# Keys two visits later, stacks loaded in parts and earlier deadlines in a hand-ordered attention stage

## The chip, the core and the metric

The kernel runs on one core of one Trainium2 chip, as one launch. The core has TensorE (PE, matrix products; its weight loads are listed as PEld), VectorE (DVE), ScalarE (ACT), GpSimd (POOL) and SyncE (SP), which here issues nearly all DMA transfers. The metric is device time in microseconds (us) of one execution. A time without the word profile is the median of several unprofiled runs; durations of single instructions come from one profiled execution.

## The reference: two spectral layers and two banded attention layers

A sequence of 2048 rows with 640 features passes through four residual layers: spectral, attention, spectral, attention. Each first normalises its input row by row.

- A spectral layer multiplies by the 640x640 cosine and sine matrices, then by the 2048x2048 ones, and keeps the real part.
- An attention layer computes queries, keys and values with one 640x1920 weight (32 heads of 20 features), scores scaled by 20^-0.5, a band mask (a row sees itself and the 255 rows before it), a softmax, the product with the values, and a 640x640 output product.

```python
x = x + _A_ref(_layernorm(x, axis=-1), ...)
x = x + _B_ref(_layernorm(x, axis=-1), B_wqkv, B_wo)
x = x + _A_ref(_layernorm(x, axis=-1), ...)
x = x + _B_ref(_layernorm(x, axis=-1), B_wqkv, B_wo)
# in _B_ref:
mask = (idx[:, None] - idx[None, :] >= 0) & (idx[:, None] - idx[None, :] < W)   # W = 256
p = _softmax(jnp.where(mask, q @ k.T * Dh ** -0.5, -1e9), axis=-1)
o = p @ v                     # then o @ wo
```

## The kernel before, in words

**Precision.** Every float32 operand is split into two float16 parts, and each product is made of three float16 products (high by high, high by low, low by high). That is why a projection of one tile is 15 matmuls: five slices of the 640 features, three products each.

**Stages.** The trace falls into four stretches: spectral layer 0 (to about 576 us), attention layer 0 (to about 1161 us), spectral layer 1 (to about 1670 us), attention layer 1 (to the end). The change touches the function `attention` (L806) and two helpers it uses.

**Blocks and visits.** Attention handles 8 blocks (b) of 256 rows. The loop at L1274 makes 128 visits, 16 to a block; visit G works on one 128-row tile and four heads. The code counts in half visits: `now[0] = 2 * G`, and r (0, 2, ... 30) is the place in the block. Below, k = r / 2 is the visit's number in its block, 0 to 15. After the last scores the loop runs on for a few tail visits, so that the delayed steps can finish.

**What one visit does**, in the order in which it is written:

1. `scores(G)` (L1090): queries by keys on PE into PSUM tile st.
2. `by_key(G - KEY_LAG)` (L1148): the transposed scores, keys by queries. They need the row maxima, which enter as two extra rows of the query stack.
3. ACT turns them into probabilities (L1171) in two halves, and POOL masks them (L1175, L1177).
4. `hand_on` (L1132), three visits after the scores of a pair: PE transposes the maxima, ACT copies them, and a DMA stores them to DRAM (htd). One visit later `take_tops` (L1142) loads them into the query stack: `qs<-htd` in the trace (`ks<-htd` for block 0, whose query stack lies in a buffer of that name).
5. `largest` (L1112): DVE masks the scores and takes the row maxima.
6. `values` (VALUE_LAG behind, L1184) and `back` (BACK_LAG behind, L1205): the product with the values, and the transposition back.
7. At the visit's end `run_unit` (L1035) runs one unit of filler work on PE, and a second one on some odd visits.

**Units** (L1003) are the projections that the stage needs anyway, one product of 15 matmuls each. Ten "qk" units make queries and keys of the next block (128x256 results, "narrow", in the trace `pf<-early,big` with 256 columns), four "v" units make the values of a block and four "out" units make the output product of a finished one (128x320 results, "wide", `pf<-big,early` and `pf<-bo,ot`). `next_unit` (L1016) prefers wide units on even visits and narrow ones on odd, then the earliest due; but when `2 * left() >= MUST_TO - r`, only units that the block must still finish come into question: its own values and the next block's queries and keys (`must`, L1066). L1333 runs a second unit on odd visits when `2 * left() > MUST_TO - r`, which is always so from r = 26 on, since MUST_TO is 26.

**Stacks.** The keys (KS) and the queries (QS) of a block lie as tall stacks in SBUF. A finished qk product is stored to DRAM (qkd) through `hold`, HOLD half visits later. After the fifth product of a stack, `load_stack` is held in the same way; it takes a buffer and calls `fill_stack` (L310): two small loads of constant rows (`onesd`, 16 KB each), then six loads of 160 KB from qkd. Key stacks share three large buffers with the first query stack (tag quad, L213), query stacks have two (L828). A buffer is free once the last `by_key` that reads it has run.

**Rows.** For each block the normalised rows are made ahead: `x<-x2d` loads two tiles, `rows_norm` (L969) normalises them in small steps (`slow_step`, at most three in two visits), and `rows_turn` (L979) transposes them by DMA into `proj.rows` (`early<-xs`). Units that need them count as ready TURN_LAG half visits after the issue. Finished outputs are turned likewise (`ot<-os`).

**Order.** While `in_turn` is set, matmuls on PE and loads on SP keep the order in which they are written (L118, L178). SP works through its queue in that order: a DMA that waits holds up every later one.

The lags and limits stand as constants at L44 to L57.

Of the kernel before, what the change touches and what calls it, by code (L numbers as in the profile page):

```python
# [40 lines left out]
LAST_STEPS = (1, 258)  # L41
LAST_FROM = 3
HAND_LAG = 3
KEY_LAG = 6  # L44
VALUE_LAG = 9
BACK_LAG = 10
STEPS = ((1, 2), (0, 2))
MUST_TO = 26
HOLD = 4
PIECES = 2  # L50
TURN_LAG = 8
UNIT = 384
ROOT = float(0x5F3759DF - (1 << 22) - (1 << 30))
M_UP = 2.0 ** 15
SHIFT = -20.0
TURN_STEPS = 8
NORM_STEPS = (0, 4)  # L57
ROW_STEPS = 3
STAGES = ((2, 4, 5, 6), (1, 3, 5, 6), (1, 3, 5, 6))
X_UP = 2.0 ** 10  # L60
# [8 lines left out]
def body(ctx: ExitStack, tc: tile.TileContext, x_in, cmat, whid, wqkv, wo, out):  # L69
# [237 lines left out]
    def new_stack():  # L307
        return new_quad("ks").bitcast(F16).rearrange("p (a b) -> p a b", a=NP)

    def fill_stack(t, b, w):  # L310

        for pi in range(2):
            load(t[64 * pi:64 * pi + 2], ones_d[w].rearrange("a (p t) -> a p t", p=NP))
        for pi in range(2):
            for r, part in enumerate((0, 1, 0) if w == 0 else (0, 0, 1)):
                v = qk_d[b][w][part].rearrange("(p two d) t -> two d p t", two=2, d=DH)[pi]
                r0 = 64 * pi + 2 + DH * r  # L320
                load(t[r0:r0 + DH], v)
# [51 lines left out]
    def spectral(layer, res_src, hidden, first):  # L373
        with ExitStack() as st:
# [359 lines left out]
            for r in range(NR):  # L734
# [22 lines left out]
                for j in range(NJ):  # L757
                    n = r * NJ + j
                    if first:
                        if (r, j) == (0, 1):  # L760
                            side.append(chain(keep_w(), b_max()))
                        if (r, j) == (1, 2):
                            side.append(chain(b_scale(), b_split(0, 15)))
                    if r == NR - 1 and j == 3:
                        early_qk = ahead(proj)
                        side.append(early_qk)
                    if r == NR - 1 and j == NJ - 1:
                        for _ in early_qk:
                            pass
                        RES[r, j] = load_res(r, j)  # L770
                        for k in (1, 0):
                            proj.stack[k] = new_stack()
                            fill_stack(proj.stack[k], 0, k)
# [12 lines left out]
                    with ExitStack() as order:  # L786
                        if j == 0 and r == 0 and first:
                            order.enter_context(tc.issue_after(hidden.last))
                        main_a(r, j)
                        if j:  # L790
                            main_c(r, j - 1)
                        main_b(r, j)
                    if r < NR - 1 and j in STAGES[r]:
                        k = STAGES[r].index(j)
                        s = RS * (r + 1) + k
                        turned_x(s)
                        if k < RS - 1:
                            turn_x(s + 1, 2)
                        z_stage(s)
# [6 lines left out]
    def attention(layer, proj, dst, final):  # L806
        with ExitStack() as st:
# [13 lines left out]

            KS, QS = {0: proj.stack[1]}, {0: proj.stack[0]}

            def load_stack(b, w):
                if w:
                    t = KS[b] = new_stack()
                else:
                    t = QS[b] = sb.tile([P, NP, QB], F16, tag="qs", name="qs", bufs=2)  # L828
                fill_stack(t, b, w)

            def proj_qk(b, w, ct):
                yield from proj.qk(b, w, ct)
                if ct == ND - 1:
                    hold(partial(load_stack, b, w))

            def proj_v(b, ti, n):
                j = 2 * b + ti
                if n == 0:
                    t = sb.tile([P, H * VS + 32 - VS], F32, tag="v", name="v", bufs=6)
# [74 lines left out]
                    yield from next_layer(i, x3)  # L914

            pieces = iter(())
            held = deque()

            def hold(f):
                held.append((now[0] + HOLD, f))  # L920

            def run_held(upto):
                while held and held[0][0] <= upto:
                    held.popleft()[1]()

            proj.held = hold
            slow, idle, handed, later = deque(), deque(), deque(), []

            def new_xs():
                while len(later) > 1:  # L930
                    later.pop(0)[1]()
                return keep.tile([P, 2, D], F16, tag="xs", name="xs", bufs=2)

            def run_later():
                while later and later[0][0] <= now[0]:
# [18 lines left out]
            def split_wo():  # L954
# [5 lines left out]
                for n in range(ND):  # L960
                    f, sc = fs.pop(0), wsc[:, 1:2]
                    nc.scalar.activation(bo[0][:, n], f, AF.Copy, scale=sc)
                    nc.vector.scalar_tensor_tensor(bo[1][:, n], f, sc, bo[0][:, n], op0=OP.mult, op1=OP.subtract)
                    if n + 2 < ND:
                        fs.append(keep.tile([P, D], F32, tag="res1", name="wst", bufs=2))
                        load(fs[-1], wo[:, n + 2])
                    yield

            def rows_norm(b, x2s):  # L969

# [45 lines left out]
            def next_unit(wide=None):  # L1016
                us = [u for u in fill if u.ready()]
                if not us:
                    return None
                if 2 * left() >= MUST_TO - now[0] % (2 * NP):  # L1020
                    us = [u for u in us if must(u)] or us
                us = [u for u in us if u.wide == wide] or us
                u = min(us, key=lambda u: u.due)
# [42 lines left out]
            def must(u):  # L1066
                b = now[0] // (2 * NP)
                return u.kind in (("v", b), ("qk", b + 1))

            def left():  # L1070
                return sum(must(u) for u in fill)
# [202 lines left out]
            for G in range(NS // 2 + 1):  # L1274
# [100 lines left out]
```

## Time and profile before

| what | value |
|---|---|
| median of 3 runs | 2233.31 us (2225.26 to 2235.92) |
| profiled execution, its own time | 2228.98 us |
| its span, first to last instruction | 2227.0 us |
| PE busy | 2041.7 us, 92% of the span |
| DVE, ACT, POOL busy | 1504.3, 1127.9, 1451.9 us |
| mean granted TensorE clock | 0.978 |

The page of the profile gives the busy time of each engine, the chain of work that ended last and the costliest groups of instructions. Further views of the same trace are used below: the waits of one engine by what ended them, the instructions in order of time, and the busy time in chosen stretches. A row such as `PE st L122 <- DMA qs<-qkd: 20.1, 9, 4.5` reads: PE, about to write st, stood idle until the DMA that fills the query stack from qkd had landed; 20.1 us in 9 waits, the longest 4.5 us. In a row of the timeline, `x15` is a run of 15 like instructions, and the square bracket is the idle time ahead of it with what ended it.

### The profile page before, as it was taken

The page shows a single profiled execution, that of the slowest core. Times are in us where ns is not written, and L with a number is a line of the kernel's source. Part 1 is how long each engine was busy: PE and PEld are TensorE (multiplying, and loading weights), DVE is VectorE, ACT ScalarE, POOL GpSimd, SP SyncE. Part 2 cuts the span into 40 slices and gives each one's busy share as a digit, 9 for nine tenths or more (in the row PEclk, how much of TensorE's full clock was granted, in tenths as well). Part 3 has the DMA queues.
Part 4 walks back from the last instruction along what each step waited for, and adds up shares of the span by engine and source line. Part 5 has one row for each costly group of instructions (what it writes and reads, how often), then busy time and mean ns, then how long its engine had stood idle before and what let it go on. Part 6 is the DMA issues. An engine that isn't in the chain of part 4 may idle for free.

```text
span 2227.0 us, 54358 instructions
## 1 busy us (share of the span) xinstructions
PE 2041.7 (92%) x21145; PEld 1475.5 (66%) x21145; DVE 1504.3 (68%) x3253; ACT 1127.9 (51%) x1971; POOL 1451.9 (65%) x2170
## 2 busy tenths in 40 slices
PE   7999999999979989988899999999998899989987
PEld 4667666767656666666666767767675666666754
DVE  8877768676757777655637767776856666667653
ACT  5444455443346666555554444443324565656644
POOL 5667688769446776655557777676765665667644
PEclk9999999999999999999999999999999899999999
DMA  7555565374544444344435455444754244453332
GB/s 252 188 199 171 181 214 198 145 287 149 128 88 106 115 101 102 88 94 93 134 122 174 149 167 173 158 165 167 267 147 94 66 95 97 107 119 75 82 70 61
DMA packets 280502, 311.00 MB, mean 140 GB/s; under 512 B 107572, under 2 KB 214836, under 8 KB 271156
## 3 DMA queue, kind: packets, MB, share of 16 engines
q1 hardware_dynamic: 279668, 306.88, 47.2%
q8 instruction: 165, 2.70, 0.5%
q14 instruction: 93, 0.76, 0.1%
q10 hardware_dynamic: 576, 0.66, 0.1%
HBM read 201.72 MB, written 83.46 MB: 128 GB/s over the span
## 4 chain that ended last, share of the span: by engine, by line
PE 58%; DVE 17%; DMA 11%; ACT 5%; issue 4%; POOL 3%; SPq 1%; DVEq 0%; POOLq 0%; ACTq 0%
PE pf L122 25%; PE y L122 10%; PE st L122 8%; PE x L122 7%; PE z L122 7%; DVE cc L521 4%; DMA qs<-qkd 4%; DVE m L1121 4%; ACT ptq L1171 3%; DMA qs<-htd 2%; DVE st L1120 2%; SPq L182 1%; DMA qkd<-early 1%; DMA res<-accd 1%; DVE lnt L147 1%
## 5 line engine op out<-in xcount | busy, mean ns | idle before, releaser
L122 PEld LDWEIGHTS <-cc 128*128 128x128 f16 x5376 | 524.6, 98 | 206.9 <-issue 6.8
L1171 ACT ACTIVATE ptq<-st,shift,alpha 128x768 f32<-128x768 f32 (+2 forms) x512 | 485.3, 950 | 295.3 <-PE st L122 243.0
L122 PEld LDWEIGHTS <-big 128*128 128x128 f16 x4320 | 421.8, 99 | 162.0 <-issue 57.5
L1120 DVE COPY_PREDICATED st<-mask,st 128x256 f32<-128x256 int32 x448 | 190.1, 424 | 280.7 <-PE st L122 276.9
L1121 DVE TENSOR_REDUCE m<-st 128x2 f32<-128x512 f32 (+1 forms) x512 | 342.7, 671 | 10.5 <-DVE r L1219 0.3
L122 PE MATMUL pf<-early,big 128*128 128x256 f16 x2400 | 296.0, 277 | 5.7 <-ACT ht L1138 5.3
L122 PE MATMUL pf<-big 128*128 128x320 f16 x1680 | 242.1, 302 | 26.5 <-DVE zc L280 16.5
L122 PE MATMUL y<-zc,cc 128*128 128x320 f16 x1728 | 262.8, 299 | 3.7 <-DVE pf L544 3.7
L1175 POOL TENSOR_SCALAR_AFFINE_SELECT ptq<-ptq 128x512 f32<-128x512 f32 x224 | 145.4, 649 | 138.2 <-ACT ptq L1171 137.9
L521 DVE SCALAR_TENSOR_TENSOR cc<-cs,cc 128x512 f16<-128x512 f32 x256 | 229.3, 903 | 0.0
L518 ACT ACTIVATE cc<-cs 128x512 f16<-128x512 f32 x256 | 149.1, 621 | 133.2 <-POOL cs L511 61.1
L122 PE MATMUL st<-ks,qs 62*128 62x128 f16 (+1 forms) x2016 | 132.5, 240 | 81.4 <-ACT ptq L1171 36.7
L1177 POOL TENSOR_SCALAR_AFFINE_SELECT ptq<-ptq 128x512 f32<-128x512 f32 x256 | 165.3, 646 | 51.2 <-ACT ptq L1171 51.2
L521 DVE SCALAR_TENSOR_TENSOR cc<-cq,cc 128x512 f16<-128x512 f32 x192 | 198.0, 1033 | 0.2 <-ACT cc L518 0.2
L122 PE MATMUL pf<-ptq,v 128*32 128x128 f32 (+1 forms) x3840 | 188.1, 335 | 0.4 <-DVE early L280 0.4
L122 PEld LDWEIGHTS <-qs 62*128 62x128 f16 x2016 | 86.0, 95 | 141.9 <-issue 125.6
L122 PE MATMUL z<-zc,cc 128*128 128x320 f16 x1152 | 177.7, 299 | 1.7 <-DVE res L544 1.7
L122 PE MATMUL x<-zc,cc 128*128 128x320 f16 x1152 | 178.8, 300 | 0.0
L1222 POOL CAST os<-o 128x160 f16<-128x160 f32 x128 | 42.2, 329 | 198.5 <-DVE o L1220 198.4
L585 POOL TENSOR_TENSOR res<-res,pf 128x320 f32<-128x320 f32 x64 | 78.1, 1220 | 137.2 <-DVE pf L544 132.8
L122 PE MATMUL pf<-big,early 128*128 128x320 f16 x960 | 147.1, 309 | 1.2 <-ACT ht L1138 1.1
L122 PEld LDWEIGHTS <-ks 62*128 62x128 f16 x3008 | 113.9, 97 | 47.8 <-issue 46.0
(135 smaller groups left out, 3363.7 us busy)
## 6 DMA issues: line engine op xcount, KB each, us to landing
cq<-in_cmat_dram SPq DMA_DIRECT2D x64, 1024.0 KB
accd<-res SPq DMA_DIRECT2D x96, 320.0 KB
res<-accd SPq DMA_DIRECT2D x96, 320.0 KB
x<-x2d SPq DMA_DIRECT2D x64, 320.0 KB
qkd<-early SPq DMA_DIRECT2D x160, 128.0 KB
ks<-qkd SPq DMA_DIRECT2D x108, 160.0 KB
qs<-qkd SPq DMA_DIRECT2D x84, 160.0 KB
x2d<-res SPq DMA_DIRECT2D x32, 320.0 KB
```

The costliest lines, as they stand in the source:

```text
L122: i = getattr(nc.tensor, what)(*args, **kw)
L147: ts(u, g, g, h, op0=OP.mult, op1=OP.mult)
L182: i = nc.sync.dma_start(out, in_)
L518: nc.scalar.activation(cc[m][:, 0], f, AF.Copy, scale=C_UP)
L521: nc.vector.scalar_tensor_tensor(cc[m][:, 1], f, C_UP, cc[m][:, 0], op0=OP.mult, op1=OP.subtract)
L585: nc.gpsimd.tensor_tensor(x1[:, hi], x1[:, hi], p1, op=OP.add)
L1120: nc.vector.copy_predicated(sp[:, :, 2 * P:3 * P], mask[:, None, :].to_broadcast([P, 2, P]), far)
L1121: topped[0] = nc.vector.tensor_reduce(TOP[n][:, pi, :, k], sp[:, :, c0:3 * P], axis=AX.X, op=OP.max).ins
L1171: nc.scalar.activation(o[:, pi], tps[pi][:, :, first * P:3 * P], AF.Sigmoid, bias=shift, scale=alpha[:, 0:1])
L1175: nc.gpsimd.affine_select(out=q[:, :, a0], in_=q[:, :, a0], pattern=[[0, 4], [-1, P]], base=0, channel_multiplier=1, compare_op=OP.is_gt, ...
L1177: ins = nc.gpsimd.affine_select(out=q[:, :, a0 + 2], in_=q[:, :, a0 + 2], pattern=[[0, 4], [1, P]], base=0, channel_multiplier=-1, compare ...
L1222: nc.gpsimd.tensor_copy(hi, o)
```

## The change

Lags and deadlines move, the loads of a stack are split, and some steps change place:

- KEY_LAG, VALUE_LAG and BACK_LAG grow by 2 (to 8, 11 and 12 visits). `hand_on` keeps its lag of 3, so the maxima have four visits instead of two between the issue of their load and their use. The last `back` of each layer comes two visits later.
- HOLD falls from 4 to 2 half visits; MUST_TO falls from 26 to 24, and to 20 in block 0 (FIRST_TO). The second unit on odd visits now needs a unit that must still be done.
- `fill_stack` is split: `ones_stack` takes the buffer and loads the constant rows; it is held from the first product of a stack on. `load_stack` only loads the six parts. Both are held until visit 8 of the block for stacks of blocks 3 to 7, and not for blocks 1 and 2. `run_held` runs every held step that is due, not only the first in line.
- TURN_LAG falls from 8 to 6. The x2 rows are loaded at visit 13 of the block before, `rows_norm` starts at visit 0 instead of 2, and the next rows' buffer is taken at visit 7 instead of 8.
- The v units of the next block are ready from the start of the block instead of from visit 8 on.
- In the last block of attention layer 0, the next layer's weights are fetched from visit 5 instead of 8 on.
- Buffers: v tiles 8 instead of 6; xs tiles 3 instead of 2, in another pool. `split_wo` spreads its steps.

```diff
-KEY_LAG = 6
-VALUE_LAG = 9
-BACK_LAG = 10
+KEY_LAG = 8
+VALUE_LAG = 11
+BACK_LAG = 12
-MUST_TO = 26
-HOLD = 4
+MUST_TO = 24
+HOLD = 2
+FIRST_TO = 4
-TURN_LAG = 8
+TURN_LAG = 6
-NORM_STEPS = (0, 4)
+X2_STEP = 26
+ROWS_STEP = 14
+HIDDEN_STEP = 10
...
-    def fill_stack(t, b, w):
+    def fill_ones(t, w):
         for pi in range(2):
             load(t[64 * pi:64 * pi + 2], ones_d[w].rearrange("a (p t) -> a p t", p=NP))
+
+    def fill_stack(t, b, w):
...
-            def load_stack(b, w):
+            def ones_stack(b, w):
                 if w:
                     t = KS[b] = new_stack()
                 else:
                     t = QS[b] = sb.tile([P, NP, QB], F16, tag="qs", name="qs", bufs=2)
-                fill_stack(t, b, w)
+                fill_ones(t, w)
+
+            def load_stack(b, w):
+                fill_stack((KS if w else QS)[b], b, w)
 
             def proj_qk(b, w, ct):
+                if ct == 0:
+                    hold(partial(ones_stack, b, w), 2 * NP * (b - 1) + 2 * KEY_LAG if b > 2 else 0)
                 yield from proj.qk(b, w, ct)
                 if ct == ND - 1:
-                    hold(partial(load_stack, b, w))
+                    hold(partial(load_stack, b, w), 2 * NP * (b - 1) + 2 * KEY_LAG if b > 2 else 0)
...
-            def hold(f):
-                held.append((now[0] + HOLD, f))
+            def hold(f, at=0):
+                held.append((max(now[0] + HOLD, at), f))
 
             def run_held(upto):
-                while held and held[0][0] <= upto:
-                    held.popleft()[1]()
+                for item in [h for h in held if h[0] <= upto]:
+                    held.remove(item)
+                    item[1]()
...
-                if 2 * left() >= MUST_TO - now[0] % (2 * NP):
+                if 2 * left() >= must_to() - now[0] % (2 * NP):
...
+            def must_to():
+                return MUST_TO - FIRST_TO * (now[0] < 2 * NP)
...
-                        fill.append(Unit(2 * NP * (b - 1) + 2 * VALUE_LAG - 2, proj_v(b, ti, n), ("v", b), 2 * NP * b + 2 * VALUE_LAG, ns=15 * 136))
+                        fill.append(Unit(2 * NP * (b - 1), proj_v(b, ti, n), ("v", b), 2 * NP * b + 2 * VALUE_LAG, ns=15 * 136))
...
-                if g < NG and b < NBQ - 2:
-                    if r == NORM_STEPS[0]:
-                        x2s = [keep.tile([P, D], F32, tag="res0", name="x2", bufs=2) for t in range(2)]
-                        for t in range(2):
-                            load(x2s[t], x2_d[2 * (b + 2) + t])
-                    if r == NORM_STEPS[1]:
-                        slow.append(rows_norm(b + 2, x2s))
-                if g < NG and r == 2 * VALUE_LAG - 2 * (VALUE_LAG % 2):
+                c = b + 2 + (r > 0)
+                if g < NG and c < NBQ and (g == 0 or r == X2_STEP):
+                    x2s = [keep.tile([P, D], F32, tag="res0", name="x2", bufs=2) for t in range(2)]
+                    for t in range(2):
+                        load(x2s[t], x2_d[2 * c + t])
+                if g < NG and c < NBQ and r == 0:
+                    slow.append(rows_norm(c, x2s))
+                if g < NG and r == ROWS_STEP:
                     flush(("v", b))
                     if b < NBQ - 2:
                         proj.new_rows(b + 2)
+                if g < NG and r == HIDDEN_STEP:
                     if b == NBQ - 1 and not final:
+                        flush(("v", b))
                         hidden = Hidden(xu_d)
...
-                if G % 2 and (g >= FULL_TO or g < NG and 2 * left() > MUST_TO - r):
+                if G % 2 and (g >= FULL_TO or g < NG and left() and 2 * left() > must_to() - r):
                     run_unit()
```

More of the change, by code (lines that the diff above doesn't have):

```diff
@@ L772, in spectral @@
                             proj.stack[k] = new_stack()
+                            fill_ones(proj.stack[k], k)
                             fill_stack(proj.stack[k], 0, k)
@@ L838, in proj_v @@
                 if n == 0:
-                    t = sb.tile([P, H * VS + 32 - VS], F32, tag="v", name="v", bufs=6)
+                    t = sb.tile([P, H * VS + 32 - VS], F32, tag="v", name="v", bufs=8)
                     nc.gpsimd.memset(t[:, :H * VS].rearrange("p (h e) -> p h e", e=VS)[:, :, DH:], 1.0)
@@ L916, in attention @@
             pieces = iter(())
-            held = deque()
-            def hold(f):
-                held.append((now[0] + HOLD, f))
+            held = []
+            def hold(f, at=0):
+                held.append((max(now[0] + HOLD, at), f))
             def run_held(upto):
-                while held and held[0][0] <= upto:
-                    held.popleft()[1]()
+                for item in [h for h in held if h[0] <= upto]:
+                    held.remove(item)
+                    item[1]()
             proj.held = hold
@@ L929, in new_xs @@
             def new_xs():
-                while len(later) > 1:
+                while len(later) > 2:
                     later.pop(0)[1]()
-                return keep.tile([P, 2, D], F16, tag="xs", name="xs", bufs=2)
+                return sb.tile([P, 2, D], F16, tag="xs", name="xs", bufs=3)
             def run_later():
@@ L963, in split_wo @@
                     nc.vector.scalar_tensor_tensor(bo[1][:, n], f, sc, bo[0][:, n], op0=OP.mult, op1=OP.subtract)
+                    for _ in range(3):
+                        yield
                     if n + 2 < ND:
@@ L966, in split_wo @@
                         load(fs[-1], wo[:, n + 2])
-                    yield
             def rows_norm(b, x2s):
```

## The prediction

> **What bounds the kernel now.** I read the page first, for the engine that carries the end.
>
> ```profile
> span 2227.0 us, 54358 instructions
> PE 2041.7 (92%) x21145; PEld 1475.5 (66%) x21145; DVE 1504.3 (68%) x3253; ACT 1127.9 (51%) x1971; POOL 1451.9 (65%) x2170
> ...
> PE 58%; DVE 17%; DMA 11%; ACT 5%; issue 4%; POOL 3%; SPq 1%; DVEq 0%; POOLq 0%; ACTq 0%
> PE pf L122 25%; PE y L122 10%; PE st L122 8%; PE x L122 7%; PE z L122 7%; DVE cc L521 4%; DMA qs<-qkd 4%; DVE m L1121 4%; ACT ptq L1171 3%; DMA qs<-htd 2%; DVE st L1120 2%; SPq L182 1%; DMA qkd<-early 1%; DMA res<-accd 1%; DVE lnt L147 1%
> ```
>
> PE leads, and 11% of the chain that ended last is DMA: the loads of the query stacks (qs<-qkd) and of the maxima (qs<-htd), which the change moves. What these cost PE itself is read from the waits of PE in the two attention stages; first stage 0 (575 to 1112 us), then stage 1 (1669 to 2190 us). Columns: total us, times, longest.
>
> ```profile
> PE st L122 <- ACT ptq L1171: 17.0, 25, 2.0
> PE st L122 <- DMA qs<-qkd: 16.3, 7, 3.0
> PE st L122 <- DMA qs<-htd: 11.0, 5, 3.1
> PE st L122 <- DMA ks<-htd: 5.1, 2, 4.6
> ...
> PE st L122 <- DMA x<-x2d: 4.5, 1, 4.5
> ```
> ```profile
> PE st L122 <- ACT ptq L1171: 23.0, 38, 2.0
> PE st L122 <- DMA qs<-qkd: 20.1, 9, 4.5
> PE st L122 <- DMA qs<-htd: 7.4, 7, 1.8
> PE st L122 <- DMA ks<-htd: 1.9, 1, 1.9
> ```
>
> PE waited for DMA 36.9 us in stage 0 (16.3 + 11.0 + 5.1 + 4.5) and 29.4 us in stage 1 (20.1 + 7.4 + 1.9): 66.3 us. The wait put down to x<-x2d is one at the first scores of a block, where a stack was due too, so I count it with the stacks.
>
> Next, where in a block they lie: PE in order of time around the start of block 3 of stage 1, and at visit 12 of that block.
>
> ```profile
> 1848.14 0.62 PE L122 MATMUL st<-ks,qs 62*128 62x128 f16 x8
> 1850.48 4.25 PE L122 MATMUL pf<-big,early 128*128 128x320 f16 x30
> 1854.66 0.28 PE L122 MATMUL st<-ks,qs 62*128 62x256 f16 x1
> 1858.42 0.69 PE L122 MATMUL st<-ks,qs 62*128 62x256 f16 x8 [3.48 <-DMA qs<-qkd]
> ...
> 1907.38 0.21 PE L122 MATMUL st<-qs,ks 62*128 62x128 f16 x1 [1.27 <-DMA qs<-htd]
> ```
>
> The first scores of a block wait for its query stack, and by_key of visit 12 waits for the maxima. What follows such a wait, and what a visit without one takes, is read from the busy time by stretches (columns: length, busy time of PE, PEld, DVE, ACT, POOL, granted clock, DMA share, GB/s):
>
> ```profile
> 1858.42:1864.41 5.99, 5.99 (x38) 3.72 (x40) 2.36 (x6) 1.98 (x2) 1.99 (x4) 0.50 1.17 269
> 1864.41:1868.86 4.45, 4.45 (x69) 3.02 (x69) 2.15 (x4) 2.84 (x5) 1.17 (x3) 0.98 0.09 32
> 1868.86:1872.11 3.25, 3.25 (x41) 2.37 (x40) 2.85 (x7) 1.98 (x2) 0.99 (x5) 1.00 0.02 6
> 1872.11:1876.19 4.08, 4.08 (x68) 3.06 (x69) 3.54 (x9) 2.41 (x4) 2.42 (x6) 1.00 0.22 81
> 1876.19:1879.44 3.25, 2.85 (x41) 2.38 (x41) 2.50 (x7) 2.42 (x4) 2.37 (x8) 1.00 0.01 1
> ...
> 575.80:1112.20 536.40, 474.34 (x6366) 345.62 (x6365) 356.98 (x858) 313.91 (x500) 325.02 (x718) 0.96 0.44 102
> 1669.50:2190.40 520.90, 465.00 (x6319) 339.84 (x6318) 336.30 (x799) 302.81 (x481) 314.61 (x708) 0.96 0.40 89
> ```
>
> After the 3.48 us wait the clock stood at 0.50 and the rest of the visit took 5.99 us; the same kind of visit undisturbed takes 3.25. The other rows price a clean visit: an even one 3.25 us with a wide or a narrow unit, an odd one 4.45 with a wide and 4.08 with a narrow. An odd visit with two wide units ran from 1848.14 to 1854.66, 6.52 us. So a visit is PE's, except that an even one doesn't fall below 3.25. A whole stage of 128 visits had a mean clock of 0.96: 8% of it at half speed, some 42 us of stage time each, of which at most half, 21 us, was lost.
>
> **The change, part by part.**
>
> *Maxima, keys at 8 visits.* The load of the maxima is issued at visit 4 after the scores' pair began; its use moves from visit 6 to 8, two visits or 7.33 us (4.08 + 3.25) later. The longest such wait above is 4.6 us, so all 25.4 us go (11.0 + 5.1 + 7.4 + 1.9). What is late next is the stack load.
>
> *Stack loads.* The queue of SP in order of time, around visits 14 and 15 of block 2, and a key stack with the maxima behind it:
>
> ```profile
> 1846.71 0.38 SPq L182 DMA_DIRECT2D qkd<-early  x1
> 1847.14 0.61 SPq L182 DMA_DIRECT2D qs<-onesd  x2
> 1848.58 3.11 SPq L182 DMA_DIRECT2D qs<-qkd  x6
> 1851.79 4.20 SPq L190 DMA_TRANSPOSE ot<-os  x1
> 1856.04 0.58 SPq L182 DMA_DIRECT2D x<-x2d  x1
> 1857.12 3.21 SPq L190 DMA_TRANSPOSE early<-xs  x2
> 1860.39 1.61 SPq L182 DMA_DIRECT2D x<-x2d  x2
> ...
> 1901.84 1.33 SPq L182 DMA_DIRECT2D qs<-htd  x2
> ```
>
> The query parts were issued from 1848.58 on and PE went on at 1858.42: 9.8 us to fill a stack. They started 1.87 us after the last store; the constant rows lie in that gap, beside the store's own landing, so loading them early gains little; I take nothing.
>
> When the last narrow unit falls, I worked out by hand from the unit rules. Before, products start at visit 3 in stage 1 and the last is at visit 12; HOLD puts the load at 14. After, rows are ready from visit 0. Units must be preferred once left() >= 12 - k. In blocks 1 to 3 the last product falls at visit 11, the load at 12, two visits (7.3 us) earlier than before: those waits (3.48 us at most of the kind quoted) go. In block 0, with its limit of 10 visits, the load moves to visit 11. From block 4 on, three or four value units of the block are still open at its start, since only six visits of a block are free for wide units and eight wide ones arise; the last product is then at visit 12 and the load at 13, one visit earlier. There it stands behind two x2 loads (0.8 us each of SP by the row of 1.61), and in stage 1 also behind the two row transposes (3.21 us), because norm steps there run two per odd visit, end at visit 11 and issue at 13. In stage 0 they issue at visit 9. From visit 13 to the next block are 4.45 + 3.25 + 4.45 = 12.2 us. The load starts after product, conversion and store: with 3 to 3.5 us, and 9.8 for filling, it lands at about 13, one us late in stage 0; in stage 1 it lands near 16 to 17, four us late. With the half clock behind it (about 2.7 us by the row of 5.99, in part) I price three boundaries at 1 us in stage 0 and at 4 us in stage 1: **15 us stay**. Bounds: 0, and 6 x (7.5 + 2.7) = 61 with the two waits of the worst boundary of before, 4.47 + 3.08:
>
> ```profile
> 2126.42 0.37 PE L122 MATMUL st<-ks,qs 62*128 62x256 f16 x1 [4.47 <-DMA qs<-qkd]
> 2129.87 0.69 PE L122 MATMUL st<-ks,qs 62*128 62x256 f16 x8 [3.08 <-DMA qs<-qkd]
> ```
>
> *A hold on SP in block 1.* The key stack of block 2 has no lower limit on its time (b > 2 is false), but three large buffers hold two key stacks and the first query stack, which by_key reads until visit 7 of block 1. Its constant rows are issued at visit 2 there, so SP stands until visit 7, and the stores and loads of maxima behind it are late by a visit or so: between nothing and 5.5 us per stage (the maxima issued at 1901.84 behind a stack landed at 1907.38). With the clock I take **3.5 us each, 7 us**.
>
> *Clock.* Of the 42 us lost at most in both stages, some is lost in visits without units (below) and stays. I take **30 us** gained, bounds 20 and 42. The Trainium skill ("TensorE: Matmul & The Clock Gate", Part 1) says that half rate follows an idle window of about 3.4 us and full rate a busy one. By it the short waits of visit 12 would cost no clock, and the gain would be some 20 us in place of 30. The trace speaks against a strict threshold: behind the wait of 1.27 us at 1907.38 a narrow unit of 15 took 2.93 us in place of 1.81:
>
> ```profile
> 1903.86 1.81 PE L122 MATMUL pf<-early,big 128*128 128x256 f16 x15
> ...
> 1908.51 2.93 PE L122 MATMUL pf<-early,big 128*128 128x256 f16 x15
> ```
>
> *Units.* The second units at visit 15 go (2.07 us each, 6.52 - 4.45, in seven blocks per stage). By the hand count 6 doubles are left per stage (two in block 0, two each in blocks 5 and 6, one of them an output forced at visit 12), where 7 were. That is a gain of 2 us per stage, **4 us**. Bounds: nothing, and 14 x 2.07 = 29.
>
> *The end of each stage.* Two more tail visits with keys but no scores. Two tail visits of stage 1 are the last two rows here:
>
> ```profile
> 2179.47:2182.72 3.25, 2.41 (x53) 1.76 (x53) 2.23 (x5) 2.18 (x4) 1.62 (x3) 1.00 0.02 4
> 2190.44:2192.11 1.67, 0.88 (x16) 0.63 (x15) 1.08 (x3) 1.04 (x2) 0.63 (x4) 1.00 0.08 32
> 2192.11:2194.87 2.76, 2.09 (x46) 1.34 (x46) 0.00 (x0) 2.21 (x3) 1.99 (x4) 1.00 0.26 101
> ```
>
> That is 1.67 + 2.76 = 4.43 us a stage, **9 us** added; what the two early visits that lose their keys save is left out, with zero as its lower bound. The first row is a visit of the last block without a unit: it takes 3.25 us all the same, so those visits give nothing back.
>
> *At nothing:* buffers and split_wo, hidden by PE; TURN_LAG 6, because a turned tile is used three visits (11 us) after its issue and a transpose held SP 4.20 us; if that cover fails, it costs the difference, one to two us a block. Weights fetched earlier lie beside PE's units.
>
> **Sum:** -66.3 - 30 - 4 + 15 + 7 + 9 = -69 us. The profiled execution itself took 2229 us (2 us around its span), so 2160 us. The median shown, 2233.31, lies 4 us above; I don't add that.
>
> **Rivals.**
>
> 1. *The stacks stay late.* If filling takes 9.8 us plus what now stands ahead, the eight boundaries that I take as cleared keep their wait, 36.4 / 14 = 2.6 us each, with 1.5 of clock: +33 us, 2193. For it: the SP rows, a queue that is full just there. Against it: two visits of lead in blocks 1 to 3.
> 2. *Everything clears.* No boundary left late, no hold: 2160 - 22, with more of the clock 2130. For it: clean visits of 3.25 and 4.45 follow at once after each wait.
> 3. *Slower: x2 loads and row transposes ahead of the stack at visit 13.* If every one of the 14 boundaries is late, each costs its wait and half clock in place of the gain; the 84 us between the forecast without its boundaries (2145) and the time of before are used up at 6 us a boundary. Landing 5 us after the first scores of a block decides; at 8 us late it would be 14 x (8 + 2.7) = 150, 2295. For it: row transposes, an output's transpose (4.20 us) and x2 loads may share the last three visits. Against it: in blocks 0 to 3 the load is issued before them. The Trainium skill ("DMA: Bandwidth & Descriptors", Queues, rings and completion order) says that each DMA engine takes descriptors in ring order, which is the ground for such a delay.
> 4. *No change:* ACT and DVE take the time that PE gains, since an even visit is at 3.25 us already. About 2225. Against it: odd visits are PE's, and the waits all lay ahead of clean visits.
>
> **How the numbers follow.** Forecast (2145 to 2175) 0.50; rival 2 (2115 to 2145) 0.17; rival 1 (2175 to 2215) 0.20; no change 0.05; slower 0.08. A measurement of this kernel tells about 0.5% from no change, 11 us. Faster by more: 0.50 + 0.17 + 0.20 = 0.87. The range leaves out rivals 3 and 4 and the ends of 1 and 2: 2118 to 2208, within the bounds of the unknown terms (the clock's 42, the boundaries' 61).
>
> **What would show it.** PE's waits for qs<-htd and ks<-htd near 0; waits for qs<-qkd only ahead of blocks 5 to 7, longer in stage 1; clean blocks 2 and 3 of about 59.4 us (8 x 3.25 + 6 x 4.08 + 2 x 4.45); an SP wait on PE in block 1; a mean clock over the stages of 0.98. Waits for qs<-qkd at every boundary would make it rival 1 or 3; waits on ACT in place of DMA, rival 4; a PE wait for early<-xs or ot<-os would show a cover that I counted as there.

## The result, and the profile after

| | before | after |
|---|---|---|
| median | 2233.12 us (2225.26 to 2240.04, 12 runs) | 2233.64 us (2228.35 to 2239.91, 12 runs) |
| span of the profiled execution | 2227.0 us | 2232.0 us |
| mean granted clock | 0.978 | 0.978 |

The ratio is 1.0002, with a 95% interval of 0.9986 to 1.0019: no change that a measurement can tell. 69 us were forecast to go.

The page after; the last line is the chain of work that ended last:

```profile
span 2232.0 us, 54291 instructions
PE 2038.7 (91%) x21145; PEld 1470.8 (66%) x21145; DVE 1507.8 (68%) x3253; ACT 1127.5 (51%) x1971; POOL 1448.6 (65%) x2170
...
PE pf L125 26%; PE y L125 10%; PE st L125 7%; PE x L125 7%; PE z L125 6%; DVE cc L523 5%; DMA qs<-qkd 4%; DVE m L1134 3%; ACT ptq L1184 3%; SPq L185 2%; DVE st L1133 2%; DMA qkd<-early 2%; DMA ks<-qkd 2%; DMA res<-accd 1%; DVE lnt L150 1%
```

The maxima (qs<-htd) are gone from the chain; the query stack (qs<-qkd) is not. The waits of PE after, in attention stage 0 (575 to 1165 us) and then in stage 1 (1669 to 2232 us), as total, times, longest:

```profile
PE st L125 <- DMA qs<-qkd: 20.4, 7, 8.4
PE pf L125 <- DMA ot<-os: 5.4, 1, 5.4
...
PE st L125 <- DMA qs<-htd: 1.9, 3, 1.1
```
```profile
PE st L125 <- DMA qs<-qkd: 23.2, 8, 4.7
PE pf L125 <- DMA early<-xs: 3.9, 2, 3.1
PE pf L125 <- DMA ot<-os: 2.7, 1, 2.7
...
PE st L125 <- DMA qs<-htd: 1.1, 1, 1.1
```

Waits for the maxima fell from 25.4 to 3.0 us. Waits for the stacks did not fall: 20.4 and 23.2 us, where they were 16.3 and 20.1, the longest 8.4 us in place of 4.5. Two covers that the prediction counted on failed: turned tiles (ot<-os) and turned rows (early<-xs) now hold PE.

The same, read from stretches of the kernel after (length, busy time of PE, PEld, DVE, ACT, POOL, clock, DMA share, GB/s). The first two rows are the scores' part of each stage (first to last visit with scores), the next two are block 2 of stage 0 and of stage 1:

```profile
578.00:1104.93 526.93, 467.46 (x6321) 340.01 (x6321) 358.15 (x857) 309.42 (x495) 320.91 (x708) 0.97 0.46 104
1669.20:2187.25 518.05, 461.67 (x6262) 337.22 (x6262) 337.94 (x797) 298.83 (x476) 310.51 (x700) 0.95 0.39 88
...
701.53:761.60 60.07, 58.38 (x857) 43.76 (x856) 49.59 (x126) 41.14 (x63) 44.56 (x97) 0.99 0.42 87
1786.94:1846.90 59.96, 58.17 (x858) 43.67 (x858) 45.00 (x108) 40.51 (x62) 43.13 (x96) 0.99 0.40 85
```

Blocks 2 are as forecast. Over both scores' parts, though, PE's idle time (length less busy) went only from 118 us before to 116. What fails lies at the **boundaries**: visit 15 of a block with visit 0 of the next. Some of the seven in each stage of the kernel after (the second, the fifth and sixth of stage 0; the third, the fifth and the last of stage 1); the sum row is over all 14:

```profile
689.65:705.10 15.45, 10.10 (x108) 6.41 (x107) 5.08 (x13) 4.39 (x6) 3.77 (x10) 0.78 0.82 178
...
881.58:903.64 22.06, 10.83 (x108) 6.77 (x108) 6.13 (x14) 4.39 (x6) 5.76 (x13) 0.69 0.74 186
959.11:972.41 13.30, 9.55 (x108) 6.11 (x109) 5.72 (x13) 4.39 (x6) 5.76 (x13) 0.87 0.73 150
...
1842.51:1850.14 7.63, 7.63 (x108) 5.36 (x108) 4.66 (x11) 5.27 (x8) 4.14 (x11) 1.00 1.18 239
...
1968.71:1986.60 17.89, 9.95 (x107) 6.57 (x108) 5.72 (x13) 4.39 (x6) 5.33 (x13) 0.71 0.74 146
...
2113.51:2129.24 15.73, 10.56 (x107) 6.82 (x108) 5.72 (x13) 4.39 (x6) 5.76 (x13) 0.78 0.67 127
sum 184.63, PE 126.05 PEld 81.96 DVE 78.37 ACT 63.26 POOL 64.35; mean PE 9.00 PEld 5.85 DVE 5.60 ACT 4.52 POOL 4.60
```

A clean boundary takes 7.63 us (the row at 1842.51), so 14 would take 107. They take 184.6; before, the same 14 stretches took:

```profile
sum 194.80, PE 150.09 PEld 101.48 DVE 73.95 ACT 71.55 POOL 64.61; mean PE 10.72 PEld 7.25 DVE 5.28 ACT 5.11 POOL 4.62
```

Ten us gained, where the forecast had 194.8 - 107 - 15 = 73. And these ten are not waits: PE is busy 24 us less there, for the second units of visit 15 run elsewhere now, and its idle time grew from 44.7 to 58.6. The 63 us are most of what is missing. The two tails took some more: from the last scores to the end of the kernel it is 44.79 us after (2187.25 to 2232.04) and 36.58 before, and stage 0's end grew by 7.0 us (557.3 to 564.3 us up to the first scores of stage 1).

How a boundary gets late shows in SP's queue of the kernel after, around visit 13 of block 4 in stage 1 (visit 13 begins at 1960.98), and in what PE does then:

```profile
1963.54 2.45 SPq L185 DMA_DIRECT2D x<-x2d  x2
1966.04 3.17 SPq L193 DMA_TRANSPOSE early<-xs  x2
1969.31 0.62 SPq L185 DMA_DIRECT2D qkd<-early  x1
1971.73 3.02 SPq L185 DMA_DIRECT2D qs<-qkd  x6
```
```profile
1970.95 2.21 PE L125 MATMUL pf<-bo,ot 128*128 128x320 f16 x15
1977.85 0.37 PE L125 MATMUL st<-ks,qs 62*128 62x256 f16 x1 [4.69 <-DMA qs<-qkd]
1981.47 0.69 PE L125 MATMUL st<-ks,qs 62*128 62x256 f16 x8 [3.25 <-DMA qs<-qkd]
...
1983.32 3.35 PE L125 MATMUL pf<-big,early 128*128 128x320 f16 x15
```

The last store of the stack (qkd<-early) went out behind the x2 loads and row transposes, 8.3 us after visit 13 began, and the load 2.4 us behind it, 1.4 us before PE had nothing left (1973.16). The stack comes in two halves: a wait of 4.69 us for the first, 3.25 us for the second, and then 15 matmuls take 3.35 us in place of 2.21.

Not every late boundary has these loads ahead. The last three boundaries of each stage are all late; three of these six (the sixth and seventh of stage 0, the seventh of stage 1) have neither x2 loads nor row transposes in SP's queue from visit 13 to the load, and still took 13.3, 12.6 and 15.7 us. The queue at the last of them, where visit 13 begins at 2105.89:

```profile
2109.21 0.38 SPq L185 DMA_DIRECT2D qkd<-early  x1
2113.53 3.22 SPq L185 DMA_DIRECT2D qs<-qkd  x6
```

The last store went out 3.3 us after visit 13 began, and the load 4.3 us behind it (2.5 us behind it at the other two). With some 9.7 us to fill a stack, that is more than the 12 us from visit 13 to the next block, even without them ahead.

### The profile page after: what moved, and what is told of

Its sections match the earlier page's. It is cut to its first block, busy times and chain, and to the rows that moved or that the text cites. A ratio compares the mean times of both kernels' runs of the same rounds, so it can differ in the third digit from the quotient of the medians.

```text
span 2232.0 us, 54291 instructions
## 1 busy us (share of the span) xinstructions
PE 2038.7 (91%) x21145; PEld 1470.8 (66%) x21145; DVE 1507.8 (68%) x3253; ACT 1127.5 (51%) x1971; POOL 1448.6 (65%) x2170
## 4 chain that ended last, share of the span: by engine, by line
PE 57%; DVE 16%; DMA 11%; ACT 5%; issue 4%; POOL 3%; SPq 3%; DVEq 0%; POOLq 0%; ACTq 0%
PE pf L125 26%; PE y L125 10%; PE st L125 7%; PE x L125 7%; PE z L125 6%; DVE cc L523 5%; DMA qs<-qkd 4%; DVE m L1134 3%; ACT ptq L1184 3%; SPq L185 2%; DVE st L1133 2%; DMA qkd<-early 2%; DMA ks<-qkd 2%; DMA res<-accd 1%; DVE lnt L150 1%
## 5 line engine op out<-in xcount | busy, mean ns | idle before, releaser
L1134 DVE TENSOR_REDUCE m<-st 128x2 f32<-128x512 f32 (+1 forms) x512 | 342.5, 671 | 10.7 <-DVE st L1133 0.5
L125 PE MATMUL pf<-early,big 128*128 128x256 f16 x2400 | 289.8, 274 | 7.9 <-ACT ht L1151 4.3
L125 PE MATMUL pf<-big 128*128 128x320 f16 x1680 | 242.0, 302 | 28.3 <-DVE zc L283 16.7
L125 PEld LDWEIGHTS pf<-ptq,v 128*32 128x32 f32 x3840 | 112.6, 111 | 44.1 <-issue 3.5
## 6 DMA issues: line engine op xcount, KB each, us to landing
qkd<-early SPq DMA_DIRECT2D x160, 128.0 KB
```

Of the source, the lines that this page charges most:

```text
L125: i = getattr(nc.tensor, what)(*args, **kw)
L1134: topped[0] = nc.vector.tensor_reduce(TOP[n][:, pi, :, k], sp[:, :, c0:3 * P], axis=AX.X, op=OP.max).ins
```

## The experiments

Three theories for the late boundaries: **order** (the load stands in SP's queue behind x2 loads and row transposes), **deadline** (a last product at visit 12 is one visit too late), **hold** (with HOLD 2, SP comes to a store before POOL has converted the product, and stands: SP waited 116.4 us for POOL's early tiles after, 38.9 before). Beside them stand the shorter TURN_LAG and the lags. A ratio is to the kernel before, with its 95% interval; unless said otherwise an edit is to the kernel after.

### The lags alone, on the kernel before

```diff
-KEY_LAG = 6
-VALUE_LAG = 9
-BACK_LAG = 10
+KEY_LAG = 8
+VALUE_LAG = 11
+BACK_LAG = 12
...
-                    t = sb.tile([P, H * VS + 32 - VS], F32, tag="v", name="v", bufs=6)
+                    t = sb.tile([P, H * VS + 32 - VS], F32, tag="v", name="v", bufs=8)
```

> The kernel before with the three lags alone raised by 2 (and 8 value tiles in place of 6). If the lag does what the trace of after suggests, the 25.4 us of waits for the maxima go to under 3 us and the two stage ends grow by 8 us each: 2233 - 25 - 5 (clock) + 16 = about 2219 us. Rival, the boundary takes it: the stack loads are met with the time that the maxima gave, the waits for qs<-qkd grow from 36 to over 50 us and the time stays at 2233.

Measured: 2245.78 us, ratio 1.0040 (1.0025 to 1.0054), slower than either expectation. PE's waits for the query stacks in stage 0 and in stage 1 of this kernel:

```profile
PE st L122 <- DMA qs<-qkd: 16.7, 8, 3.7
...
PE st L122 <- DMA qs<-qkd: 36.0, 11, 7.5
```

No wait for the loads of maxima is left (one of 4.7 us is put down to a store of theirs), and the waits for stacks stand at 16.7 and 36.0 us, where they were 16.3 and 20.1. In stage 1 a visit that no longer waits for its maxima brings PE sooner to a boundary whose stack comes no sooner. Removing one of two waits in a row is worth little while the second is set by DMA. The tails are the other part: they are 10.7 and 9.2 us longer than before (568.0 and 45.8 us).

### The change without the lags

```diff
-KEY_LAG = 8
-VALUE_LAG = 11
-BACK_LAG = 12
+KEY_LAG = 6
+VALUE_LAG = 9
+BACK_LAG = 10
```

> The changed kernel with the old lags (6, 9, 10), all else as changed. If the lag is a gain, the maxima are waited for again and the ends shrink: 2234 + 25 + 5 - 16 = about 2248 us. If the longer ends eat the lag (rival), it is 2234 or below, and the waits for the maxima stay small because stacks now load at other visits.

Measured: 2250.40 us, ratio 1.0053 (1.0033 to 1.0073). PE's waits for qs<-htd in stage 0, then in stage 1:

```profile
PE st L125 <- DMA qs<-htd: 23.2, 11, 4.8
...
PE st L125 <- DMA qs<-htd: 30.1, 9, 5.2
```

With 15.3 us more for ks<-htd (9.9 and 5.4), maxima cost 68.6 us and stacks 15.1: the same exchange from the other side. Within the change the lags are worth some 11 us (1.0053 to 1.0002).

### The stack loads ahead of the x2 loads

```diff
+                if g < NG and r == X2_STEP:
+                    run_held(now[0])
                 c = b + 2 + (r > 0)
```

> The changed kernel with the held steps of visit 13 (last store, stack load) issued ahead of the x2 loads and row transposes of that visit. Order theory: the stack load of blocks 5 to 7 starts some 5 us earlier in stage 1 and 1 to 2 us in stage 0, so the 52 us lost at these six boundaries fall by about 20: 2214 us. Bandwidth theory (rival): the same bytes share the same time, the load lands as late as before, 2234 within 4 us. Third: the store then blocks SP until POOL has converted the last product, and x2 and the rows come late instead: 2234 or above, with waits for early<-xs.

Measured: 2227.07 us, ratio 0.9952 (0.9926 to 0.9979). The three late boundaries of stage 1 fell from 17.9, 16.5, 15.7 to 14.5, 13.8, 12.2 us; those of stage 0 did not (22.1, 13.3, 12.6 to 20.8, 16.5, 12.5). Order alone is worth some 11 us by the ratios (7 by the profiled executions), and leaves the boundaries late.

### TURN_LAG 8

```diff
-TURN_LAG = 6
+TURN_LAG = 8
```

> The changed kernel with TURN_LAG 8 again: units that need transposed tiles wait four visits in place of three. If the waits for ot<-os and early<-xs (8.1 and 3.9 us, with half clock behind them some 17 us) come from the shorter lag, they go: about 2219 us. Rival: the unit that no longer runs early leaves a visit empty and comes back as a second unit later, so the time stays within 5 us of 2234.

Measured: 2211.47 us, ratio 0.9878 (0.9841 to 0.9914). The waits of 5.35 and 2.68 us for ot<-os at the end of block 1 went, block 1 fell from 71.0 and 69.6 to 63.4 and 62.3 us and block 7 by about 5 in each stage. The ratios give 28 us (0.9878 to 1.0002), but the profiled execution, the slowest of the four, is only 13 us shorter than the changed kernel's (2218.7 to 2232.0): in it blocks 2 and 3 took 12 us more with the same matmuls. So the profile accounts for 13 us, and where the other 15 lie is not shown. The row of the kernel after with the wait:

```profile
697.41 4.18 PE L125 MATMUL pf<-bo,ot 128*128 128x320 f16 x15 [5.35 <-DMA ot<-os]
```

The transpose was issued at 690.92, behind a stack load (687.11, 3.77 us of SP). With TURN_LAG 8 it went out no earlier (691.21), but its unit was used later. At that boundary PE then waited 0.87 and 3.33 us for the stack instead; the one of stage 1 fell from 13.7 to 8.1 us.

### The last product a visit earlier

```diff
-MUST_TO = 24
+MUST_TO = 22
```

> The changed kernel with MUST_TO 22, so that by the hand count the last product of blocks 4 to 6 falls a visit earlier, at visit 11. If the late boundaries 4 to 7 come from the deadline, their visits 15 and 0 together fall from the 22.1, 13.3, 12.6 us of stage 0 and 17.9, 16.5, 15.7 us of stage 1 to 10 us or less each, and the time falls by 25 to 45 us, less 2 us for each second wide unit that an odd visit takes on. If the order of the queue sets them, the load still stands behind what is ahead of it, the boundaries fall by 3 us each at most, and the time stays within 10 us of the changed kernel's. If the path is full whatever the order, nothing changes.

Measured: 2183.80 us, ratio 0.9767 (0.9727 to 0.9807): 52 us less than the change. Of its six boundaries from block 4 on these are two of stage 0 and one of stage 1 (the three left out take 7.63 or 7.64 us), and the sum is over all 14:

```profile
875.82:888.65 12.83, 9.60 (x108) 6.10 (x109) 6.08 (x14) 4.38 (x6) 5.37 (x12) 0.87 0.84 172
944.66:952.29 7.63, 7.63 (x108) 5.36 (x108) 5.67 (x13) 4.38 (x6) 4.13 (x11) 1.00 0.64 153
...
1941.15:1949.43 8.28, 7.84 (x107) 5.43 (x108) 5.67 (x13) 4.38 (x6) 4.13 (x11) 1.00 1.20 207
...
sum 128.03, PE 110.49 PEld 74.59 DVE 78.33 ACT 62.17 POOL 57.86; mean PE 7.89 PEld 5.33 DVE 5.60 ACT 4.44 POOL 4.13
```

The boundaries lost 56.6 us (184.6 to 128.0), which is the gain and a little more. SP's queue of this kernel at the same place (visit 12 begins at 1930.17, the first scores were due at 1945.53):

```profile
1934.14 0.38 SPq L185 DMA_DIRECT2D qkd<-early  x1
1936.09 2.66 SPq L185 DMA_DIRECT2D qs<-qkd  x6
...
1939.96 0.90 SPq L185 DMA_DIRECT2D x<-x2d  x2
1940.90 7.00 SPq L193 DMA_TRANSPOSE early<-xs  x2
```

The load now starts 9.4 us before its stack is due, in place of 1.4, and nothing waits for it. Of these 8 us 3.2 are the visit and 4.4 are SP's: the store follows the start of its visit by 4.0 us in place of 8.3, since at visit 12 neither x2 loads nor row transposes are ahead.

### HOLD back at 4

```diff
-HOLD = 2
+HOLD = 4
```

> The changed kernel with HOLD back at 4: stores and loads are issued two visits later than with HOLD 2. If the short hold makes SP stand on POOL's conversions (116.4 us in all after, 38.9 before) and by that backs up its queue, SP's wait on POOL falls under 60 us, the row transposes and output transposes ahead of the stacks land earlier, and the boundaries stay or improve by 1 to 3 us each: the time is within 15 us of the changed kernel's. If the short hold is what gives the stacks their lead, every boundary gets later by about a visit (4 us), so 14 times 4 us at most, and the time rises by 20 to 55 us.

HOLD counts half visits, so 4 in place of 2 puts stores and loads one visit later, not two. Measured: 2280.40 us, ratio 1.0189 (1.0152 to 1.0225). SP's wait for POOL did fall, and every boundary is late (the sum row is over all 14):

```profile
SPq L185 <- POOL early L363: 36.7, 30, 6.3
```
```profile
sum 240.60, PE 140.16 PEld 89.82 DVE 81.60 ACT 63.33 POOL 72.70; mean PE 10.01 PEld 6.42 DVE 5.83 ACT 4.52 POOL 5.19
```

The products of blocks 1 to 3 fall at visit 11 as in the changed kernel, but their loads are now written at visit 13, behind the x2 loads there, and the boundaries from block 2 to 3 and from 3 to 4 take 16.2 to 19.2 us, where they took 7.6 to 9.3: one visit more is enough to make a stack late. The run moves two things at once, so it doesn't price SP's standing for POOL. With MUST_TO 22, however, SP stands as long (116.2 us) and all but one of the late six take under 8.3 us: standing alone does not make the stacks late, and as the cause of the late boundaries the hold theory falls. The short hold is worth 42 us in this change.

### MUST_TO 22 with the x2 loads a visit earlier

```diff
-MUST_TO = 24
+MUST_TO = 22
...
-X2_STEP = 26
+X2_STEP = 24
```

> MUST_TO 22 with the two x2 loads moved from visit 13 to visit 12, where they are issued ahead of the held stack loads again, as they were at visit 13 in the changed kernel. If it is the visit that counts (the time from the load to the next block's first scores), the boundaries stay clean at about 7.6 us and the time is within 8 us of MUST_TO 22 alone (2184). If it is the order, the stack again stands behind x2 loads, boundaries 4 to 7 go back towards 12 to 18 us, and the time rises by 20 us or more.

Measured: 2195.77 us, ratio 0.9821 (0.9801 to 0.9842), about 12 us behind MUST_TO 22 alone, with intervals that just touch: between the two expectations. Its boundary 4 to 5 of stage 0 and the sum:

```profile
883.56:900.86 17.30, 10.57 (x107) 6.84 (x108) 6.05 (x14) 4.40 (x6) 5.38 (x12) 0.70 0.58 122
...
sum 141.90, PE 117.47 PEld 78.14 DVE 79.77 ACT 63.43 POOL 58.58; mean PE 8.39 PEld 5.58 DVE 5.70 ACT 4.53 POOL 4.18
```

The other five of the late six are at 7.63 or 7.64. Of the six, only the two after block 4 have x2 loads at all. In stage 1 these are ahead of the stack again and cost nothing at visit 12: the store went out 4.0 us after that visit began, as without them. So there the visit decides. In stage 0, where the queue is fullest, order still costs 4 to 5 us, and 10 us more lie at the boundaries after blocks 0, 1 and 3, which were not followed up. The row transposes, which took longer than the x2 loads in stage 1, stay behind the load there; putting those ahead at visit 12 was not tried.

### Both causes together

The first kernel has TURN_LAG 8 and the stack loads ahead of the x2 loads, the second TURN_LAG 8 and MUST_TO 22.

```diff
-TURN_LAG = 6
+TURN_LAG = 8
...
+                if g < NG and r == X2_STEP:
+                    run_held(now[0])
```

> The changed kernel with TURN_LAG 8 and with a run of the held loads ahead of the x2 loads of visit 13. Measured apart, the first was worth about 22 us and the second 7 to 9 us. If the two causes are independent, they add: 29 us under the changed kernel, near 2204 us. If a turned tile's transpose and the stack's load are one queue's delay, counted twice, it stays at the 2211 us of TURN_LAG 8 alone.

```diff
-MUST_TO = 24
+MUST_TO = 22
...
-TURN_LAG = 6
+TURN_LAG = 8
```

> The changed kernel with TURN_LAG 8 and MUST_TO 22. By the theory of the deadline the boundaries of blocks 5 to 7 go as well: 25 us or more under TURN_LAG 8 alone, 2187 us or less. By the theory of the queue's order it is within 10 us of TURN_LAG 8 alone, 2201 to 2221 us.

Measured: 2205.48 us, ratio 0.9857 (0.9817 to 0.9897), and **2172.11 us, ratio 0.9705 (0.9670 to 0.9740)**. The first lies between its two expectations, and its interval overlaps that of TURN_LAG 8 alone: inconclusive. The second is faster than both kernels by 66 us by the ratios, and below the 2187 us that the deadline theory asked for. Its span is 2168.9 us, with PE busy 93% of it, where it was 92% before.

### The tails: values and outputs closer to the keys

Both are on the kernel with TURN_LAG 8 and MUST_TO 22 (2172 us): values at 10 and outputs at 11 visits, and at 9 and 10.

```diff
-VALUE_LAG = 11
-BACK_LAG = 12
+VALUE_LAG = 10
+BACK_LAG = 11
```

> TURN_LAG 8 and MUST_TO 22 with values and outputs a visit earlier (VALUE_LAG 10, BACK_LAG 11). If the longer ends of the two stages (15 us more than before) come from the lags, a visit less takes about half of what lags are for there, 2 to 4 us a stage, 4 to 8 us in all: 2164 to 2168 us. If they come from the outputs of the last blocks being done later, nothing changes but waits of the values for ACT: 2172 us or some us more.

```diff
-VALUE_LAG = 11
-BACK_LAG = 12
+VALUE_LAG = 9
+BACK_LAG = 10
```

> TURN_LAG 8 and MUST_TO 22 with keys still 8 visits behind, but values at 9 and outputs at 10 as before the change: the same parity of visits as with 11 and 12, two tail visits fewer at the end of each stage. If the tails' 15 us come from the lag of the outputs, 3 to 8 us a stage go: 2156 to 2166 us. If they come from outputs done later, the tails stay and the time is 2172. If the values, now one visit behind the probabilities in place of three, wait for ACT or POOL, each pair of visits gets longer: 0.5 us each would be 64 us, 2235.

Measured: 2238.84 us, ratio 1.0011 (0.9994 to 1.0027), and 2584.66 us, ratio 1.1561 (1.1540 to 1.1581). With 10 and 11 the tail of stage 1 fell by 3.9 us (44.4 to 40.5) and that of stage 0 by 2.8, as the lag theory asks, but the step to an even lag puts the values into the even visits. Two visits of that kernel in a row, and its largest wait in stage 0:

```profile
775.62:779.57 3.95, 3.95 (x70) 2.93 (x70) 3.14 (x8) 2.64 (x4) 3.28 (x9) 1.00 0.07 19
779.57:783.40 3.83, 3.09 (x39) 2.36 (x39) 2.79 (x9) 2.52 (x4) 2.56 (x6) 1.00 0.18 53
```
```profile
PE pf L125 <- ACT ht L1151: 40.6, 55, 1.4
```

A pair takes 7.78 us in place of 7.33 (4.08 + 3.25), some 29 us for the 64 pairs of a stage. Two stages less the shorter tails make 51 of the 68 us that the ratios give; the rest was not followed. With 9 and 10 the values come one visit after their probabilities, and PE waits for ACT in the middle of odd visits (34 such waits in stage 0, 77.9 us). In this visit it then runs on near half speed (3.24 us for the narrow unit in place of 1.81):

```profile
837.16 2.03 PE L125 MATMUL pf<-ptq,v 128*32 128x256 f32 x32 [2.59 <-ACT ptq L1184]
839.13 3.24 PE L125 MATMUL pf<-early,big 128*128 128x256 f16 x15
```

So neither shorter lag gives back the 15 us of the tails. A spacing of one visit from keys to values is too short; two visits came only together with the change of parity, so whether two would do by themselves is not shown.

## Why the prediction was wrong

- **The maxima: right.** 25.4 us became 3.0, by the lag of two visits.
- **Blocks 2 and 3: right.** 59.4 us forecast; 60.1 and 60.0 in the rows above, 61.2 for block 3 of stage 0. Block 3 of stage 1 took 64.7, with a wait of 3.1 us for early<-xs, a cover counted on.
- **The unit schedule: right.** The last product falls at visit 11 in blocks 1 to 3 and at visit 12 from block 4 on, as worked out, and the loads of blocks 5 to 7 come late just where it said.
- **The stacks of blocks 5 to 7: the step that failed.** The six boundaries were priced at 1 us each in stage 0 and 4 us each in stage 1, 15 us. They take 98.0 us where clean ones take 45.8, so the term was 52, near its upper bound of 61. PE was idle 37.9 us at the six, 18.7 for the first half of a stack and 19.2 for the second, and it was busy 14.3 us longer than at six clean ones, on the same matmuls (the half clock behind the waits). The 15 us priced the lateness of the first half alone, in sum near enough. The second half's wait (2.9 to 3.5 us at each) was left out, though the two waits of before stood in the quoted rows, and the half clock was named but not added. The 3 to 3.5 us from visit 13 to the load fit the store alone: it went out at 3.3 to 4.1 us where neither x2 loads nor row transposes were ahead, and the load stood another 2.2 to 4.3 us behind it until the store had landed, a gap that the prediction had read (1.87 us) and did not add. And SP was taken to issue the row transposes at visit 9 in stage 0, as written; its queue runs visits behind there, and in block 4 they went out in visit 12, as this row of the kernel after shows (visit 13 begins at 872.43). The load of that block was issued 16.2 us after visit 13 began, where 3 to 3.5 were assumed.

```profile
870.68 4.50 SPq L193 DMA_TRANSPOSE early<-xs  x2
...
884.93 0.38 SPq L185 DMA_DIRECT2D qkd<-early  x1
888.58 2.90 SPq L185 DMA_DIRECT2D qs<-qkd  x6
```

- **TURN_LAG 6 "at nothing": failed.** The text gave the condition (the cover of three visits, 11 us) and priced its loss at one to two us a block; undone, it gives 28 us by the ratios, of which the profile shows 13, and 14 on top of MUST_TO 22 (0.9767 to 0.9705). In block 1 the cover fell to a transpose queued behind a stack load, not to its own length.
- **Hold on SP in block 1: the mechanism right, the size not.** SP issued nothing between these rows of stage 0, 18 us, yet PE waited only 0.57 us for maxima behind it, and 1.06 in stage 1, in place of 3.5 each.

```profile
641.82 0.55 SPq L185 DMA_DIRECT2D ks<-htd  x2
659.90 0.54 SPq L185 DMA_DIRECT2D ks<-onesd  x2
```

- **Tails: 9 forecast, 15 measured** (7.0 + 8.2). A visit of lag is worth 2.8 to 3.9 us a stage, so two visits make some 7.
- **Units: 4 forecast, nothing came.** Second units run in seven visits of each stage after, where six were counted; before, it was six visits in stage 0 and seven in stage 1.
- **Clock: 30 forecast, nothing came.** The stages stand at 0.97 and 0.95, where they stood at 0.96: the waits at the boundaries were to go, and did not. With MUST_TO 22 both are at 0.98. The Trainium skill ("TensorE: Matmul & The Clock Gate", Part 1) ties half rate to an idle window of PE of about 3.4 us. The 4.18 us behind the wait of 5.35 agree with that; the 3.24 behind one of 2.59 are near half rate after a shorter wait.

Of the forecast's range, rival 3 came nearest (x2 loads and row transposes ahead of the stack at visit 13), but for all 14 boundaries. Six were late, by 8.7 us each, and at three of these six it is not the mechanism, for nothing of the kind was ahead. The forecast itself had these six boundaries as late, and had their price wrong. Rival 4 gave the right time for a wrong reason: ACT took nothing to speak of (42.2 us of waits in before's whole span, 46.9 after).

The account closes in the rough: 63 us at the boundaries (37 at the late six, 14 at the block with the failed turn, 12 at the rest), 6 in the tails, against a gap of 74 by the spans (2227 - 69 to 2232); about 5 stay unassigned. What is not settled is where 15 of the 28 us of TURN_LAG 8 lie, which no trace shows, and how much of MUST_TO 22's gain in the fullest block is order.

## What to carry to other kernels

A transfer that is moved earlier must be followed through the queue that issues it, with all that stands ahead and the landing of its own store: here one visit (3.25 us) in a deadline was worth 52 us of time, and in a block where it also passed a crowded visit, 8 us of lead. When two waits follow one another, removing the first only brings the second sooner, so price the second as the one that decides. A lag has a least size set by the engines between its two ends, and here its parity mattered too, by what the visit already does; change it by steps that keep both.

## What the runs showed of the hardware

- Two row transposes took SP 3.17 us in the kernel after and 7.00 us with MUST_TO 22, where they were issued behind a stack load still in flight.
- The stack load took 9.7 us from issue to the last half in use (1971.73 to 1981.47). The first half let PE start 3.6 us earlier, but with one matmul only: the next needed the second half.
- Slower matmuls followed waits of 2.6 to 5.4 us here: 3.24 us for 1.81 and 4.18 for 2.21, near half speed, and 3.35 for 2.21. A wait's length alone does not tell it: behind one of 2.24 us in the kernel with values at 9 the same narrow unit took 1.81, and behind one of 1.27 us before the change 2.93.
- An 18 us silence of SP cost PE about 1 us in each stage: what that stand cost was set by what was due behind it, not by its length.
